# Long convolution with real and imaginary parts on one partition, in 64x32 and 32x64 pieces of the array

## The chip, the cores and the metric

The kernel runs on one core of one Trainium2 chip. The metric is the time of one execution in microseconds (us), the median of several timed runs. A separate execution was taken by the hardware profiler; its trace and its page are what is read here.

## The reference

Two independent heads are computed and put side by side, 1024 columns each, for 2048 time steps.

Head A is a long convolution with gates:

```python
k_shift = sum over t of k_pad[:, t:t+S, :] * shift_k[:, ks-1-t]     # four taps
kv = k_shift * v
y_f = rfft(kv padded to 2S) * rfft(ssm_k padded to 2S)
y = irfft(y_f)[:S] + kv * ssm_D
a = q * y
```

Head B is a linear recurrence with a diagonal complex state:

```python
Bu = einsum("bld,pd->blp", x, B_bar)          # B_bar complex, 1024 x 1024
h  = Lam_bar * h + Bu[:, t, :]                # 2048 steps, one after the other
y  = 2.0 * einsum("blp,dp->bld", hseq, Cmat).real + x * Dskip
```

All inputs and the output are bf16.

## The kernel before, in words

**Order.** The work of both heads is cut into small tasks, and a long string, ORDER, lists every task in an order fixed beforehand: `name.arguments@engine:slots`. The loop at the end of `full_kernel` calls the tasks in that order. Each engine works through its own instructions in this order; there is no other scheduler. `@G` or `@S` sets the queue of a transfer (G for POOL's, S for SP's; `@D` and `@G` choose VectorE or GpSimd for a copy), and `:a3` or `:d0d1` name the buffers that the task takes: rings a and b in SBUF, e for the spectrum products, w for weights, m for products on VectorE; in PSUM p0 and p1 (one bank each) and d0 to d2 (two banks each). A task that takes a buffer waits until the last user of it is done.

**Head B.** B is loaded (`bl`), transposed on TensorE (`bT`, L458) and copied (`bc`); C and x come by transposing transfers (`cx` L480, `x` L483), on SP's queue. For each of 16 blocks of 128 steps: `U` (L492) multiplies x with B, `ue` copies it, `r1` (L506), `r2`, `sc` (the scan, L523), `r3`, `r4` run on VectorE, `y` (L546 and L551) multiplies with C and D, `ye` and `yst` bring it out. `cm` carries the state from block to block.

**Head A.** The convolution of 4096 points is a product of a transform of 128 points and one of 32. Sequence positions are laid out as 128 partitions x 16 rows.
- `kp` and `vp` load k and v; `kvm`, `kva`, `kvb`, `kvc` make kv on VectorE.
- `am` (L610) is kv's first stage: for row r and half u one matmul per half of the columns, with the 128x128 block matrix F1t, half of which is zero (the two interleaved halves of the sequence do not mix). `ae` copies, `ast` writes to the DRAM array Ys_kv.
- `hl`, `hT`, `hc`, `hm` (L643), `he`, `hst` do the same for the filter ssm_k, into Ys_h.
- For each of 16 groups gq: `lh`, `lk` load the groups back in another layout. `sh` and `sk` (`s2`, L676) are the second stage, four pieces of 64 rows x 64 columns each; `she` and `ske` copy to hab and x16. Real and imaginary parts of a frequency lie on different partitions, 32 apart. `sw` exchanges these halves of hab with four transfers from SBUF to SBUF. `pr` (L704) multiplies on VectorE: x16 with hab and with the exchanged hab. `sa` (L717) is the inverse, again in pieces of 64x64, two accumulated for each result; `sae` copies, `vst` writes to the DRAM array Vs.
- `vl` loads rows of Vs, `a3` (L744) is the output stage with Gt (two accumulated matmuls for each half of the columns), `a3e` copies, `qm` multiplies with q (`qp` loads it), `ost` writes out.

Of the kernel before, what the change touches and what calls it, by code (L numbers as in the profile page):

```python
# [16 lines left out]
BF16 = mybir.dt.bfloat16  # L17
# [10 lines left out]
def a_constants():  # L28
# [4 lines left out]
    G1 = np.zeros((2, 2, 32, 2, 64, 2))  # L33
    for h in range(2):
        F1[:, h, :, h] = np.transpose(F, (0, 2, 1, 3))
        G1[h, :, :, :, :, h] = np.transpose(F, (1, 3, 2, 0)) * (2 / NFFT)
# [5 lines left out]
    WF = np.zeros((2, N2, 2, 32, 3, N2))  # L42
# [3 lines left out]
    WF[:, :, :, :, 2, :] = WF[:, :, :, :, 0, :]  # L46
    WI = np.zeros((2, 2, N2, 16, 2, 2, N2, 2))
    for gi in range(2):
        for ui in range(2):
            for gq in range(16):  # L50
                cc = np.transpose(c_[ui, 2 * gq + gi], (1, 0)); ss = np.transpose(s_[ui, 2 * gq + gi], (1, 0))
                o = WI[gi, :, :, gq, ui]
                o[0, :, 0, :, 0] = cc; o[0, :, 0, :, 1] = ss
                o[1, :, 0, :, 0] = -cc; o[1, :, 0, :, 1] = -ss
                for cp in range(2):
                    o[cp, :, 1, :, 0] = -ss; o[cp, :, 1, :, 1] = cc
    W = np.concatenate([WF.reshape(128, NWP, 4 * 96), WI.reshape(128, NWP, 2 * 256)], axis=2)
    f = lambda a: np.ascontiguousarray(a.reshape(128, -1), dtype=np.float32).astype(ml_dtypes.bfloat16)
    return f(F1), f(G1), f(W)
# [3 lines left out]
NA = 11  # L63
# [6 lines left out]
wb.7:p1 bc.5.1 par_rest vp.0@G:a10 ld_G@S sin2 wb.4:p0 cx.5.1 wbe.4 sin1 wb.6:p0 cx.0.0 wbe.6@D eo.0 bl.3.1:b3 wb.1:p0 wbe.7@D bl.1.0:b4 wbe.1@D  # L70
wb.2:p1 cx.0.1 eo.1 stt.0 wb.0:p0 cx.7.0 wbe.2 stt.1 eo.3 wb.5:p1 bl.3.0:b6 x.1:b2 wbe.5@D wbe.0 stt.3 wb.3:p1 wbe.3 bT.6.1:p0 cx.1.0 dd bT.2.0:p1
kvm.0:m0 vp.1:a1 vp.2:a0 cx.6.0 bc.6.1 cx.6.1 bT.0.1:p0 bc.2.0 bc.0.1@D kp.2@G eo.2 bT.2.1:p1 kva.0 hT.0.0:p0 hc.0.0:b8 stt.2 bc.2.1 hT.0.1:p0
bT.7.1:p1 hc.0.1:b13 kvb.0:a7 bc.7.1 hT.0.6:p0 hm.0.0.1:d0 kvc.0 hc.0.6:b10 hT.0.3:p1 hm.0.0.0:d1 kvm.4:m0 he.0.0.1:b5 am.1.1:d2 hc.0.3:b11
hm.0.6.1:d0 hst.0.0.1 hT.0.2:p0 bT.0.0:p1 he.0.6.1:b8 hc.0.2:b0 hst.0.6.1@S cx.1.1 bc.0.0 bT.7.0:p0 bc.7.0@D cx.3.1 z1 U.0.3.0:p1 kva.4 hm.0.6.0:d0
U.0.3.1 cx.3.0 U.0.2.0:p0 kvb.4:a8 U.0.2.1 ue.0.3:a10 he.0.6.0:b7 kvm.2:m0 bT.1.0:p1 bc.1.0 am.0.1:d0 bT.3.0:p1 ue.0.2 bc.3.0 bT.3.1:p0 bc.3.1
U.0.0.0:p1 U.0.0.1 he.0.0.0:b5 kp.4@G kva.2 kp.3@G ae.0.1:b10 hm.0.3.1:d1 U.2.2.0:p0 ue.0.0 ast.0.1@S vp.4:a5 kvc.4 U.0.1.0:p1 ae.1.1:b4 cx.5.0
hm.0.1.0:d0 he.0.3.1:b6 ast.1.1 kvb.2:a6 hm.0.3.0:d2 hst.0.6.0 U.0.1.1 he.0.1.0:b3 hst.0.3.1 kvc.2 U.2.2.1 ue.0.1 hst.0.1.0 he.0.3.0:b11 U.1.2.0:p1
r1.0:m0 ue.2.2:a0 hst.0.3.0@S hm.0.1.1:d1 hst.0.0.0@S am.4.0:d0 he.0.1.1:b8 cx.2.0 U.2.1.0:p0 r2.0:a1 U.1.2.1 U.2.1.1 ue.1.2:a10 kvm.8:m0 U.1.1.0:p1
ue.2.1 ae.4.0:b13 hm.0.2.0:d2 am.4.1:d1 z2 ast.4.0 am.0.0:d0 U.2.3.0:p0 hst.0.1.1 ae.4.1:b4 U.1.1.1 he.0.2.0:b7 ast.4.1@S sc.0 U.2.3.1 ue.1.1
hst.0.2.0@S hm.0.2.1:d1 cx.7.1 ue.2.3 am.5.1:d2 ae.0.0:b6 hT.0.4:p1 cx.2.1 am.2.0:d0 hc.0.4:b10 ast.0.0 U.1.0.0:p0 ae.2.0:b3 hT.0.7:p1 cx.4.0 kva.8  # L80
U.1.0.1 ue.1.0 hT.0.5:p0 hc.0.7:b0 hl.5:a9 kvb.8:a4 hl.4:a2 U.2.0.0:p1 hc.0.5:b13 ast.2.0@S hl.7:a3 r3.0:m0 U.1.3.0:p0 he.0.2.1:b8 am.1.0:d0 hst.0.2.1
hm.0.5.0:d1 U.1.3.1 cm.0:a7 kvc.8 U.2.0.1 ue.1.3 he.0.5.0:b11 r4.0 U.4.0.0:p0 ue.2.0 hm.0.4.0:d1 r1.1:m0 U.4.0.1 he.0.4.0:b5 U.4.2.0:p1 ue.4.0:a5
hst.0.4.0@S ae.5.1:b6 hm.0.7.1:d1 r2.1 U.4.2.1 ae.1.0:b4 ast.5.1 U.4.1.0:p0 hl.6@G:a10 r1.2:m0 he.0.7.1:b7 ast.1.0@S hst.0.5.0 am.8.1:d2 ue.4.2
U.4.1.1 hm.0.5.1:d0 sc.1 am.5.0:d1 he.0.5.1:b8 U.4.3.0:p1 ue.4.1 am.2.1:d0 ae.5.0:b3 y.0.0.0:p0 ae.2.1:b13 hm.0.4.1:d1 hm.0.7.0:d0 ast.2.1@S U.4.3.1
x.3:b6 he.0.7.0:b10 r2.2:a0 am.8.0:d0 ae.8.1:b5 hst.0.7.0 y.0.0.1 r3.1:m0 hst.0.5.1 ue.4.3 ast.8.1@S ast.5.0@S y.0.0.2 ae.8.0:b0 vp.3:a8 y.0.1.0:p1
ast.8.0 cm.1 hst.0.7.1 r4.1 am.3.0:d2 y.0.1.1 ae.3.0:b4 r1.4:m0 y.0.0.3 ast.3.0 ye.0.0:b11 hT.1.4:p0 y.0.1.2 sc.2 hc.1.4:b13 he.0.4.1:b10 hT.1.3:p0
hm.1.4.1:d0 am.9.0:d2 hc.1.3:b9 hst.0.4.1@S ae.9.0:b8 hT.1.5:p0 am.9.1:d1 y.0.1.3 he.1.4.1:b5 r2.4:a5 am.3.1:d2 ye.0.1 hst.1.4.1 hm.1.3.1:d0
y.1.1.0:p1 he.1.3.1:b0 kvm.6:m0 hc.1.5:b3 y.1.1.1 hst.1.3.1@S ae.3.1:b7 hT.1.7:p0 y.1.1.2 ae.9.1:b4 hm.1.4.0:d0 hm.1.5.1:d2 hc.1.7:b10 ast.9.1 y.1.1.3
kp.6 kva.6 hT.1.6:p0 ast.9.0@S ye.1.1:b5 kp.5 hm.1.7.0:d1 hc.1.6:b13 yst.0@S y.1.0.0:p1 ast.3.1@S he.1.5.1:b0 hT.1.1:p0 cm.2:a4 kvb.6:a1 y.1.0.1
hst.1.5.1 hc.1.1:b4 lw.1@G:w0 hm.1.6.0:d2 r3.2:m0 y.1.0.2 he.1.6.0:b2 y.1.0.3 he.1.4.0:b8 hst.1.6.0@S hT.1.0:p0 r4.2 ye.1.0 hst.1.4.0 hm.1.6.1:d2  # L90
hm.1.3.0:d0 he.1.6.1:b13 vp.6@G:a6 U.3.2.0:p1 kvc.6 yst.1 he.1.7.0:b9 hst.1.6.1 hm.1.1.0:d2 kvm.12:m0 U.3.2.1 hc.1.0:b0 hst.1.7.0@S x.7:b11
hm.1.7.1:d1 y.2.0.0:p0 he.1.7.1:b10 x.6:b7 he.1.1.0:b8 y.2.0.1 hm.1.0.0:d1 hst.1.1.0@S hm.1.1.1:d2 he.1.0.0:b2 y.2.0.2 kva.12 ue.3.2:a7 am.6.1:d1
# [54 lines left out]
def full_kernel(ctx, tc, A_q, A_k, A_v, A_shift_k, A_ssm_k, A_ssm_D, B_x, B_Lre, B_Lim, B_Bre, B_Bim,  # L147
# [235 lines left out]
    def kv_space():  # L383
# [45 lines left out]
    def kx(b):  # L429
        nc.sync.dma_start_transpose(st["kT"][:, b, 4:4 + S], k[:, b * P:(b + 1) * P])  # L430
# [393 lines left out]
```

## Time and profile before

| | |
|---|---|
| median of 3 timed runs | 385.99 us (381.66 to 388.22) |
| profiled execution, its own time | 380.41 us |
| its span, first to last instruction | 378.5 us |
| granted TensorE clock | 1.000 |
| busy: TensorE, VectorE, ScalarE, GpSimd | 92%, 86%, 70%, 21% |
| DMA packets, bytes | 67418, 100.06 MB |
| U (L492), y (L546), one-block-of-D (L551) | 127.7, 127.7, 28.0 us busy on TensorE |
| hm (L643), am (L610), a3 (L744) | 20.6, 19.0, 16.1 us |
| second stage (L676), inverse (L717) | 256 matmuls each; 22.1 and 18.2 us |
| transposes of B and of the filter (L458, L630) | 13.9, 12.5 us |

How to read it: PE is TensorE's matmuls, PEld its weight loads, DVE VectorE, ACT ScalarE, POOL GpSimd, SP SyncE, which only issues transfers here. A matmul's busy time contains its way through the pipeline: of matmuls that follow each other, the starts tell the pace, not the durations. Where a row names a releaser ("<-DMA ld"), the engine sat idle until this had come.

### The profile page before, as it was taken

Reading aid. Unit: us, or ns where it says so; the run is one execution under the profiler, and the core shown is the slowest. Engines: PE = TensorE matmul, PEld = TensorE weight load, DVE = VectorE, ACT = ScalarE, POOL = GpSimd, SP = SyncE. Lnnn points to the kernel's source line nnn. Section 1 sums busy time; section 2 is a strip of 40 time slices with the busy share of each in tenths; the row PEclk is TensorE's granted clock in tenths of the full one; section 3 lists DMA queues with packets and bytes.
Section 4 is the critical chain, followed back from the end, with each engine's and each line's share of the span. In section 5 each row is a group of like instructions: output and inputs, shape, how many; then the busy total and the mean of one; then the engine's idle time right before and its main releaser. Section 6 shows DMA issues by size and latency. Waiting matters only on the chain.

```text
span 378.5 us, 8748 instructions
## 1 busy us (share of the span) xinstructions
PE 346.6 (92%) x3661; PEld 225.6 (60%) x3661; DVE 324.6 (86%) x229; ACT 264.2 (70%) x341; POOL 81.3 (21%) x150
## 2 busy tenths in 40 slices
PE   4548889899899999999999999989999999999995
PEld 3226678785455578855444757367867664467442
DVE  6989599999999997999997797576899999993972
ACT  4978798877778886952785879778869771346433
POOL 7300023022112521214200325330210202211021
PEclk9999999999999999999999999999999999999999
DMA  6999999997578999999999897999989539877995
GB/s 231 317 338 216 265 272 286 296 314 235 200 243 270 247 313 287 281 272 268 190 275 312 258 324 234 220 267 221 284 236 312 175 125 325 306 229 255 350 319 206
DMA packets 67418, 100.06 MB, mean 264 GB/s; under 512 B 38435, under 2 KB 42147, under 8 KB 67380
## 3 DMA queue, kind: packets, MB, share of 16 engines
q1 hardware_dynamic: 54660, 56.32, 54.8%
q0 software_dynamic: 12720, 43.19, 36.8%
q8 instruction: 28, 0.46, 0.5%
q14 instruction: 10, 0.08, 0.1%
HBM read 49.16 MB, written 33.55 MB: 219 GB/s over the span
## 4 chain that ended last, share of the span: by engine, by line
PE 56%; DMA 15%; issue 13%; ACT 7%; SPq 4%; POOL 2%; DVE 1%; POOLq 0%; ACTq 0%; DVEq 0%
PE ps_u L492 22%; PE ps_y L546 16%; PE ps_a L744 4%; DMA wts<-a_c_W 4%; SPq L483 4%; DMA Ys_kv<-ysb 3%; PE ps_a L643 3%; DMA l2k<-Ys_kv 3%; DMA ld<-in_B_B_re_dram 3%; PE ps_a L717 3%; PE ps_a L610 3%; DMA hab<-hab 2%; PE ps_a L676 2%; PE ps_t L630 2%; ACT ysb L615 2%
## 5 line engine op out<-in xcount | busy, mean ns | idle before, releaser
L492 PEld LDWEIGHTS <-BT 128*128 128x128 bf16 x2048 | 119.3, 98 | 22.6 <-issue 11.7
L492 PE MATMUL ps_u<-xT,BT 128*128 128x128 bf16 x2048 | 127.7, 219 | 2.4 <-ACT u L497 1.2
L546 PE MATMUL ps_y<-CT,h 128*128 128x512 bf16 x512 | 127.7, 379 | 0.0
L546 PEld LDWEIGHTS <-h 128*128 128x128 bf16 x512 | 44.6, 98 | 48.0 <-issue 6.1
L523 DVE TENSOR_TENSOR_SCAN h<-rtab,h 128x2080 bf16<-128x2080 f32 x16 | 71.8, 4488 | 0.2
L497 ACT CAST u<-ps_u 128x512 bf16<-128x512 f32 x64 | 38.2, 603 | 27.0 <-PE ps_u L492 19.1
L506 DVE TENSOR_TENSOR mt<-u,Z 128x4096 bf16<-128x4096 bf16 x16 | 36.7, 2291 | 15.8 <-ACT u L497 15.4
L704 DVE TENSOR_TENSOR hab<-x,hab 128x4096 bf16<-128x4096 bf16 x16 | 36.5, 2286 | 15.2 <-DMA hab<-hab 10.5
L556 ACT CAST yo<-ps_y 128x512 bf16<-128x512 f32 x32 | 19.1, 596 | 28.0 <-PE ps_y L546 24.4
L650 ACT CAST ysbh<-ps_a 128x1024 bf16<-128x1024 f32 x32 | 32.3, 1033 | 8.8 <-PE ps_a L643 7.5
L691 ACT CAST x<-ps_a 128x1024 bf16<-128x1024 f32 x32 | 31.9, 1026 | 8.8 <-PE ps_a L676 5.9
L506 DVE TENSOR_TENSOR mt<-h,Z 128x4096 bf16<-128x4096 bf16 x16 | 36.7, 2292 | 0.5
L724 ACT CAST vsb<-ps_a 128x1024 bf16<-128x1024 f32 x32 | 31.7, 1027 | 6.5 <-PE ps_a L717 6.0
L583 DVE TENSOR_TENSOR mt<-kring,wbc 128x2048 bf16<-128x2048 bf16 (+3 forms) x14 | 35.8, 2592 | 0.4 <-ACT wbc L473 0.2
L615 ACT CAST ysb<-ps_a 128x1024 bf16<-128x1024 f32 x32 | 32.3, 1043 | 2.7 <-issue 1.6
L685 ACT CAST hab<-ps_a 128x1024 bf16<-128x1024 f32 x32 | 32.2, 1030 | 2.1 <-PE ps_a L676 1.9
L551 PE MATMUL ps_y<-Dd,xT 128*128 128x128 bf16 x128 | 28.0, 219 | 0.0
L749 ACT CAST ot<-ps_a 128x1024 bf16<-128x1024 f32 x16 | 15.7, 1018 | 14.1 <-PE ps_a L744 14.1
L169 POOL DMA_DIRECT2D Ys_h<-ysbh x20 | 14.3, 716 | 43.3 <-ACT ysbh L650 43.3
L168 POOL DMA_DIRECT2D hab<-hab x32 | 15.6, 494 | 32.1 <-ACT hab L685 18.3
L458 PE MATMUL ps_t<-ident,ld 128*128 128x128 bf16 x128 | 13.9, 285 | 9.1 <-DMA ld<-in_B_B_re_dram 4.4
L643 PE MATMUL ps_a<-hT,F1t 128*128 128x512 bf16 x64 | 20.6, 402 | 0.8 <-ACT ysbh L650 0.6
(116 smaller groups left out, 381.8 us busy)
## 6 DMA issues: line engine op xcount, KB each, us to landing
Ys_h<-ysbh POOLq DMA_DIRECT2D x20, 256.0 KB, 5.5
l2h<-Ys_h SPq DMA_DIRECT2D x9, 512.0 KB, 9.7
Vs<-vsb SPq DMA_DIRECT2D x9, 512.0 KB, 4.3
vv<-Vs SPq DMA_DIRECT2D x9, 512.0 KB, 5.2
Ys_kv<-ysb POOLq DMA_DIRECT2D x17, 256.0 KB, 6.2
l2k<-Ys_kv SPq DMA_DIRECT2D x8, 512.0 KB, 3.9
hab<-hab SPq DMA_DIRECT2D x32, 128.0 KB, 5.4
l2k<-Ys_kv POOLq DMA_DIRECT2D x8, 512.0 KB, 7.8
```

Source lines behind the costliest of these rows:

```text
L492: nc.tensor.matmul(pu[:, w, jl, :], BT[:, 2 * jp + jl, w, d, :], xT[:, d, :], start=(d == 0), stop=(d == ND - 1))
L497: nc.scalar.copy(u[:, :, 2 * jp:2 * jp + 2, :], st["pu", i, jp][:])
L506: nc.vector.tensor_mul(m, s_, w_)
L523: nc.vector.tensor_tensor_scan(gf, rtab[:].rearrange("p a j t -> p (a j t)"), gf, 0.0, ALU.mult, ALU.add)
L546: nc.tensor.matmul(py[:], h[:, 1 - w, j, 2:TP], CT[:, j, w, dh * 512:(dh + 1) * 512], start=(j == 0 and w == 0), stop=(j == NJ - 1 and w = ...
L583: nc.vector.tensor_mul(m[:, :, j0:j0 + n, :], a_, wbc[:, j0:j0 + n, :].unsqueeze(1).to_broadcast([P, 2, n, DV]))
L615: nc.scalar.copy(st["ysb", r, u][:], st["pa", r, u][:].rearrange("p e d -> p (e d)"))
L643: nc.tensor.matmul(pd[:, e, :], F1t[:, u, :], st["hT", f, rp][:, e, :], start=True, stop=not sk)
L650: nc.scalar.copy(st["yh", f, rp, u][:], st["pa", f, rp, u][:])
L685: nc.scalar.copy(hab[:, a, :, e * 512:(e + 1) * 512], st["ps", key, gq, e][:])
L691: nc.scalar.copy(x16[:, :, e * 512:(e + 1) * 512], st["ps", "k", gq, e][:])
L704: nc.vector.tensor_mul(hab, x16.unsqueeze(1).to_broadcast([P, 2, 2 * D]), hab)
```

## The change

- **Layout of the sequence.** Position n*32 + h*16 + s lies on partition 64h + n (before: 2n + h), for k, v, q and the output. The transfers of k, v, q take rows of 4 KB as before; the two early tasks `kp.-1` and `kp.-2` are cut at 64 and 63 partitions instead of 112 and 15.
- **kv's first stage.** `am` does both halves u and both halves h of the sequence for half the columns, as four pieces of 64x64 (FK is the new part of F1t, without zeros). `ysb` is one tile for a row r now, with 4 KB a partition, in ring a; `ast` is split by h instead of u.
- **Second stage.** `s2` makes one part (ri: real or imaginary) for all columns, in eight pieces of 64 rows x 32 columns. The real and the imaginary part of a frequency then lie on the same partition. There is no `sw`.
- **Product.** `pr` multiplies the two parts of hab with the two parts of x16, four products of 1024 elements: as many elements as before.
- **Inverse.** `sa` makes both halves of the columns at once, in four steps of eight pieces of 32 rows x 64 columns, and takes two of the buffers d0 to d2. The weights have three blocks instead of two (wts: 1024 columns instead of 896).
- **Output stage.** `a3` has, for each half of the columns, two matmuls of 128 rows x 64 columns side by side instead of two accumulated ones of 128x128. `vl` is split in two transfers.
- **Order.** The whole of ORDER is new, with one more buffer in ring a (NA = 12). Which copies go to VectorE, and which transfers to which queue, changes with it.

```diff
-NA = 11
+NA = 12
...
-ld_par bl.4.0@G:b0 bl.5.0@G:b1 bl.5.1@G:b2 bl.4.1:b3 bl.6.0:b4 bl.2.1@G:b5 ld_sd@S bl.1.1@G:b6 ld_w@S:a0a1 kp.0@G kp.-2 ld_F par_T:p0 hl.2@G:a2
-bl.7.0:b7 bT.4.0:p1 p32 exp1 bl.6.1:b8 hl.3@G:a3 bc.4.0 dve2 x.0:b9 kp.-1@G bT.5.0:p0 dve3 sm_pre bT.4.1:p1 bc.5.0 hl.1@G:a4 bl.0.1:b10 bc.4.1
-bl.7.1@G:b11 x.4:b12 bT.6.0:p0 tabA1:a5a6a7a8 bc.6.0 bl.2.0:b13 hl.0:a9 exp2 bl.0.0:b0 sin0 rt@G kp.1 bT.1.1:p1 x.2:b1 bT.5.1:p0 tabA2 bc.1.1 cx.4.1
+ld_par bl.2.0@G:b0 bl.4.1@G:b1 ld_F bl.0.1:b2 ld_sd@S:b3 bl.2.1@G:b4 hl.3:a0 bl.5.1@G:b5 ld_w@S:a1a2 bl.7.0@G:b6 kp.-1 hl.1@G:a3 par_T:p0 bl.6.0@G:b7
+bl.7.1:b8 bT.2.0:p1 p32 bl.5.0:b9 bl.4.0@G:b10 exp1 cx.4.1 dd dve2 kp.-2@G dve3 bc.2.0@D kp.0@G bl.1.1:b11 sm_pre hl.0@G:a4 bT.2.1:p0 hl.2@G:a5
...
-    kr = k.rearrange("(n s) d -> n s d", s=NR)
+    kr = k.rearrange("(n h s) d -> h n s d", h=2, s=NR)
...
-    def am(r, u):
+    def am(r, e):
         pd = dtile("ps_a")
-        st["pa", r, u] = pd
-        for e in range(2):
-            nc.tensor.matmul(pd[:, e, :], F1t[:, u, :], kvt(r)[:, r % 2, e * 512:(e + 1) * 512], start=True, stop=True)
+        st["pa", r, e] = pd
+        for h in range(2):
+            hp = slice(64 * h, 64 * h + 64)
+            for u in range(2):
+                nc.tensor.matmul(pd[64 * u:64 * u + 64, h, :], F1t[hp, 256 + 64 * u:320 + 64 * u],
+                                 kvt(r)[hp, r % 2, e * 512:(e + 1) * 512], start=True, stop=True, tile_position=(64 * h, 64 * u))
...
-    def s2(key, nm, gq, e, o):
+    def s2(key, nm, gq, ri):
...
         for gi in range(2):
-            for u in range(2):
-                up = slice(64 * u, 64 * u + 64)
-                b0 = ((2 * gq + gi) % 4) * 96 + 32 * o
-                nc.tensor.matmul(pd[64 * gi:64 * gi + 64, u, :], wt[up, b0:b0 + 64],
-                                 st[nm, gq][up, gi, e * 512:(e + 1) * 512], start=True, stop=True,
-                                 tile_position=(64 * u, 64 * gi))
+            b0 = ((2 * gq + gi) % 4) * 64 + 32 * ri
+            for e in range(2):
+                c_ = 32 * (2 * gi + e)
+                for u in range(2):
+                    up = slice(64 * u, 64 * u + 64)
+                    nc.tensor.matmul(pd[c_:c_ + 32, u, :], wt[up, b0:b0 + 32], st[nm, gq][up, gi, e * 512:(e + 1) * 512],
+                                     start=True, stop=True, tile_position=(64 * u, c_))
...
-    def sw(gq):
-        hab = st["hab", gq]
-        for b in range(4):
-            o = b ^ 1
-            spd(hab[32 * b:32 * b + 32, 1, :, :], hab[32 * o:32 * o + 32, 0, :, :])
-    E["sw"] = sw
...
     def pr(gq):
-        hab = st["hab", gq][:].rearrange("p a u d -> p a (u d)")
-        x16 = st["x16", gq][:].rearrange("p u d -> p (u d)")
-        nc.vector.tensor_mul(hab, x16.unsqueeze(1).to_broadcast([P, 2, 2 * D]), hab)
+        hab = st["hab", gq][:].rearrange("p a b u d -> p a b (u d)")
+        x16 = st["x16", gq][:].rearrange("p b u d -> p b (u d)")
+        nc.vector.tensor_mul(hab, hab[:, :, 1:2, :].to_broadcast([P, 2, 2, D]), x16.unsqueeze(1).to_broadcast([P, 2, 2, D]))
...
-    def sa(gq, e):
+    def sa(gq):
         wt = st["w", gq // 2]
         hab = st["hab", gq]
-        pd = dtile("ps_a")
-        st["ps", "v", gq, e] = pd
-        for a in range(2):
-            for u in range(2):
-                for gi in range(2):
-                    gp = slice(64 * gi, 64 * gi + 64)
-                    b0 = 4 * 96 + (gq % 2) * 256 + u * 128 + a * 64
-                    nc.tensor.matmul(pd[64 * u:64 * u + 64, gi, :], wt[gp, b0:b0 + 64],
-                                     hab[gp, a, u, e * 512:(e + 1) * 512], start=(a == 0), stop=(a == 1),
-                                     tile_position=(64 * gi, 64 * u))
+        pds = [dtile("ps_a") for _ in range(2)]
+        for a, b, n in ((0, 0, 0), (0, 1, 2), (1, 0, 2), (1, 1, 1)):
+            for gi in range(2):
+                for e in range(2):
+                    st["ps", "v", gq, e] = pds[e]
+                    cp = slice(32 * (2 * gi + e), 32 * (2 * gi + e) + 32)
+                    for u in range(2):
+                        b0 = 4 * 64 + (gq % 2) * 384 + u * 192 + n * 64
+                        nc.tensor.matmul(pds[e][64 * u:64 * u + 64, gi, :], wt[cp, b0:b0 + 64], hab[cp, a, b, u, :],
+                                         start=(a + b == 0), stop=(a + b == 2), tile_position=(32 * (2 * gi + e), 64 * u))
...
-    def vl(r):
-        st["vv", r] = k4("vv", [P, 2, D])
-        spd(st["vv", r][:], Vs[:, r, :, :].rearrange("u k d -> k u d"))
+    def vl(r, h):
+        vv = once(("vv", r), lambda: k4("vv", [P, 2, D]))
+        spd(vv[:, h, :], Vs[:, r, 64 * h:64 * h + 64, :])
...
         for e in range(2):
-            for u in range(2):
-                nc.tensor.matmul(pd[:, e, :], Gt[:, u, :], st["vv", r][:, u, e * 512:(e + 1) * 512], start=(u == 0), stop=(u == 1))
+            for h in range(2):
+                nc.tensor.matmul(pd[64 * h:64 * h + 64, e, :], Gt[:, h, :], st["vv", r][:, h, e * 512:(e + 1) * 512],
+                                 start=True, stop=True, tile_position=(0, 64 * h))
```

More of the change, by code (lines that the diff above doesn't have):

```diff
@@ L52, in a_constants @@
                 o = WI[gi, :, :, gq, ui]
[L53 to L57, printed above, removed]
+                o[:, :, 0, :, 0] = cc; o[:, :, 0, :, 1] = ss
+                o[:, :, 1, :, 0] = -cc; o[:, :, 1, :, 1] = -ss
+                o[:, :, 2, :, 0] = -ss; o[:, :, 2, :, 1] = cc
@@ L73 @@
[L73 to L80, printed above, removed]
@@ L657, in lw @@
     def lw(w):
-        st["w", w] = rtile(ring, "w", "wts", [P, 4 * 96 + 2 * 256])
+        st["w", w] = rtile(ring, "w", "wts", [P, 4 * 64 + 2 * 384])
         spd(st["w", w][:], Wv[:, w, :])
@@ L686, in full_kernel, with she, ske @@
+    E["sh"] = lambda gq, ri: s2("h", "l2h", gq, ri)
+    E["sk"] = lambda gq, ri: s2("k", "l2k", gq, ri)
+    def she(gq, ri):
+        hab = once(("hab", gq), lambda: k8("hab", [P, 2, 2, 2, 512]))
+        nc.scalar.copy(hab[:, ri, 1, :, :], st["ps", "h", gq, ri][:])
     E["she"] = she
-    E["sxe"] = lambda gq, e: she(gq, e, "x", 1)
-    def ske(gq, e):
-        x16 = once(("x16", gq), lambda: k4("x16", [P, 2, D]))
-        nc.scalar.copy(x16[:, :, e * 512:(e + 1) * 512], st["ps", "k", gq, e][:])
+    def ske(gq, ri):
+        x16 = once(("x16", gq), lambda: k4("x16", [P, 2, 2, 512]))
+        nc.scalar.copy(x16[:, ri, :, :], st["ps", "k", gq, ri][:])
```

215 lines of the change are left out of this document (110 added, 105 removed).

## The prediction

> **What bounds the kernel now.** I read the page first (busy time by engine, chain of waits), then the windows, then the timeline of TensorE where it changes between whole-array and piece work, then the timeline at the start.
>
> ```profile
> PE 346.6 (92%) x3661; PEld 225.6 (60%) x3661; DVE 324.6 (86%) x229; ACT 264.2 (70%) x341; POOL 81.3 (21%) x150
> ```
> TensorE is busy for 92% of the span. The windows (length, then busy time and instructions of PE, PEld, DVE, ACT and POOL, the granted clock, the DMA share and GB/s) tell where the other 8% lie:
>
> ```profile
> 0.00:10.00 10.00, 4.11 (x33) 3.34 (x33) 6.97 (x22) 5.17 (x6) 7.11 (x19) 1.00 0.69 237
> 10.00:20.00 10.00, 5.36 (x22) 2.32 (x23) 9.43 (x29) 9.09 (x18) 3.45 (x7) 1.00 1.05 310
> 20.00:30.00 10.00, 5.05 (x37) 3.63 (x37) 8.26 (x12) 7.69 (x21) 0.53 (x1) 1.00 1.15 339
> 30.00:40.00 10.00, 8.72 (x50) 5.10 (x49) 9.53 (x10) 6.88 (x8) 0.74 (x1) 1.00 1.08 219
> 40.00:50.00 10.00, 7.92 (x106) 6.79 (x105) 6.09 (x4) 8.41 (x10) 0.00 (x0) 1.00 1.14 276
> ...
> 250.00:300.00 50.00, 47.55 (x709) 35.56 (x707) 42.51 (x21) 40.71 (x51) 6.75 (x13) 1.00 0.93 255
> 300.00:350.00 50.00, 49.86 (x459) 29.91 (x456) 41.43 (x25) 24.83 (x33) 7.83 (x12) 1.00 0.69 233
> ```
> In the first 50 us TensorE works 31.2 us (the sum of the five rows) and idles 18.8. From 50 to 350 us it idles 9.3 us in all (the six windows of 50 us). So what counts is how much TensorE work there is, how early it can start, and a few waits in between. A group of the page that the change touches (busy time, mean ns, idle time before it and what ended it):
>
> ```profile
> L704 DVE TENSOR_TENSOR hab<-x,hab 128x4096 bf16<-128x4096 bf16 x16 | 36.5, 2286 | 15.2 <-DMA hab<-hab 10.5
> ```
> And four pieces of the chain of waits (start, duration, what):
>
> ```profile
> 205.42 0.56 PE ps_a L676 x8
> ...
> 207.84 0.99 PE ps_a L717 x16
> ...
> 213.62 0.77 PE ps_a L676 x12
> ...
> 323.38 0.86 PE ps_a L744 x4
> ```
> A full-array matmul of 512 columns takes a place of 0.216 us (four in 0.86). Pieces of 64x64 take the same place four at a time: 8, 12 and 16 of them last 0.56, 0.77 and 0.99 us, that is 0.216 us for each round of four and 0.126 us over. Ahead of a stretch of pieces the trace has another gap: the last U matmul starts at 205.202, its successor would start 0.056 later, the first piece starts at 205.351, which is 0.093 us more; nearly all 34 visits show this 0.093. So a visit to piece work costs 0.219 us, plus 0.216 us a round.
>
> **The change, part by part.** The sum is made against the profiled execution: 380.41 us, of which the span is 378.5; it lies 1.4% under the median of the timed runs, 385.99, so that a result of the sum is multiplied by 1.0147 at the end.
>
> (1) First stage of kv (am, L610). Before: 64 matmuls in place of 0.216 = 13.8 us. After: 128 pieces of 64x64 = 32 rounds = 6.9 us. The built order of the changed kernel puts them in 28 visits (24 of one round, 4 of two): 28 x 0.219 = 6.1 us. Sum -0.8 us: alone in its visit, one am costs 0.435 us against 0.432. Nearly nothing is won.
>
> (2) Output stage (a3, L744). Before 64 x 0.216 = 13.8 us. After, 64 matmuls of 128 rows by 64 columns, two column halves at a time if they run as the 64x64 pieces with the same rows do (these start 2 to 4 ns apart): 32 places = 6.9 us, and 16 visits = 3.5 us. Sum -3.4 us. If they don't run together: +3.5 us. I take -3.4, since two column halves side by side are what the pieces of L676 are already.
>
> (3) Second stages (L676) and inverse (L717). Before: 512 pieces in fours = 128 rounds = 27.6 us, and 39 visits in the built order = 8.5 us. After: 1024 pieces (64x32 and 32x64), by eights again 128 rounds, and 42 visits (26 and 16) = 9.2 us. Sum +0.7 us if eight run at once, as four do; +27.6 more if only four do (13.8 for each of the two kinds). No row shows more than four at once. The nearest is the round itself: starts 1.6 to 3.5 ns apart, and the next round 0.216 later, so issue leaves room for eight (8 x 3.5 = 28 ns). What is not seen is four streams into the same rows, and four accumulators written at the same time. I take eight at once.
>
> The Trainium skill (TensorE: Matmul & The Clock Gate, Part 3: Packing small matmuls) says that small tiles run concurrently, about 4 ns a tile, up to sixteen. By that page the term is +0.7, by the row's cautious reading +28.3; no run here shows eight yet.
>
> (4) The exchange goes. 64 transfers of 128 KB (8.4 MB of the page's 100 MB) leave the queues: 32 from SP, 32 from POOL (15.6 us of issue there). VectorE waited 10.5 us for them in four products, but it is not the bound: TensorE lost 0.7 us to the product behind it, 2.3 to weights (wts) and 0.7 to l2h loads that shared the DMA. The product keeps its size and its 2.29 us (both operands are repeated, as in the r1 products of L506, 2.29 us too). ScalarE's copies keep count and size; only three copies of BT (0.69 us each) go to VectorE and two of wbc to ScalarE. Of those 3.7 us I take 2 as won: -2 us; the ends are -9 (all idle time of 50 to 350) and +16.5, from the next point.
>
> (5) The inverse now holds two of the three big accumulators at once (before one), and each is freed by a ScalarE copy of 1.03 us. Behind it in TensorE's order stand mostly U and y matmuls, which use the small accumulators, so I take 0. If each of the 16 waited for one copy: 16 x 1.03 = +16.5 us; for both, +33. Queued behind such a wait is everything on TensorE.
>
> (6) The new order at the start, where the trace shows this (SP's queue and TensorE's waits):
>
> ```profile
> 6.99 4.90 SPq L483 DMA_TRANSPOSE xT<-in_B_x_dram  x1
> ...
> 12.71 8.41 SPq L483 DMA_TRANSPOSE xT<-in_B_x_dram  x1
> 21.17 0.58 SPq L168 DMA_DIRECT2D ld<-in_B_B_re_dram  x1
> ```
> ```profile
> 11.70 1.89 PE L458 MATMUL ps_t<-ident,ld 128*128 128x128 bf16 x16 [2.48 <-DMA ld<-in_B_B_im_dram]
> ...
> 26.83 1.89 PE L458 MATMUL ps_t<-ident,ld 128*128 128x128 bf16 x16 [3.68 <-DMA ld<-in_B_B_re_dram]
> ```
> Two x transposes keep SP's queue for 13.3 us, B loads stand behind them, and TensorE waits 2.5 and 3.7 us for B. The changed order has 7 transposes ahead of the first U matmul (before 14: 4 of x, 10 of C), and 12.3 MB of transfers instead of 14.5. At the mean 286 GB/s of 10 to 50 us, 2.1 MB are 7.4 us; the two waits are 6.2 us. But POOL's queue now has 17 transfers ahead of the first product of kv instead of 12 (0.53 us each, +2.7), and the last three B loads stand behind the table copies (2.0 us) and four other loads, so U of step 0 may wait for them. I take -5 us; the ends are -12 and +3.
>
> Other parts: k, v, q and output rows are still pieces of 4 KB or 2 KB, and vv loads are split in two (16 issues of about 0.5 us more, in the last third, where the DMA share is 0.69): 0. The weights grow from 224 to 256 KB a load: 0.25 MB in all: 0.
>
> **Sum**: -0.8 - 3.4 + 0.7 - 2 - 5 = -10.5 us: 369.9 us in a profiled execution, 375 us as a median, 2.8% under before.
>
> **Rivals.** (B) The start and the transfers give more: -3.5 - 10 - 6 = -19.5, 366 us. For it: DMA share over 1.0 from 10 to 50 us. Against: after 50 us little idle time is left to win. (C) Start and transfers give nothing, as the products of kv on VectorE (9.43 and 9.53 us busy in two of the first windows) hold it back: -3.5, 382 us. (D) The other side: eight pieces do not run at once. It decides from 82 ns more a round on (10.5 us / 128 rounds); at four at a time for both kinds it is -10.5 + 27.6 = +17.1: 403 us, for one kind 389. Against it: issue leaves room; for it: nothing in the trace shows four streams a row. (E) The pair of accumulators: +16.5 to +33 as in (5), net +6 to +22, middle 400 us. For it: in 250 to 300 us TensorE already idles 2.45 us and ScalarE is busy 81%; against: the order has other work between. That the change does not do what it says gets no chance: the built program has no exchange, and the counts are those above.
>
> **How the numbers follow.** The measurement of this kernel tells about 2% from no change (its three runs differ by 1.7%). The forecast has 0.46, with its own range 366 to 384 (0.39 faster, 0.07 within 2%); B 0.12 (faster); C 0.12 (0.08 within 2%, 0.04 slower with a late B load on top); D 0.15 (0.12 slower, 0.03 within, one kind only); E 0.15 (0.12 slower, 0.03 within). That is 0.51, 0.21, 0.28. The range 362 to 396 holds the forecast, C, most of B and the lower ends of D and E.
>
> **What would show it.** Right: rounds of eight 0.216 us apart in L681 and L713; a3 0.65 us in a visit; first U before 40 us (44.1 before); PE busy about the same while the span is shorter. Wrong: a distance of 0.3 us or more between rounds (D); TensorE waiting for copies of vsb ahead of L713 (E); first U at 44 us or later (C).

## Result and profile after

The changed kernel takes 676.72 us (median of 4 runs, 665.95 to 684.48); the kernel before, beside it on the same chip, takes 383.83 us (378.63 to 388.22). The ratio is 1.761, 95% interval 1.711 to 1.812. Executions of one kernel fall into a fast and a slower group a few per cent apart, and every ratio with an interval compares the fast ones alone, so it can differ a little from the ratio of two medians. The forecast was 375 us, 2.8% faster: 302 us short. The profiled execution took 684.48 us where the sum for it said 369.9. Its first U matmul starts at 85.0 us (44.1 before).

The page of the changed kernel, busy time and the DMA's packets, queues and chain:

```profile
PE 392.7 (58%) x4237; PEld 239.6 (35%) x4237; DVE 325.8 (48%) x230; ACT 264.1 (39%) x340; POOL 97.4 (14%) x146
...
DMA packets 99729, 92.22 MB, mean 135 GB/s; under 512 B 72885, under 2 KB 76997, under 8 KB 99686
...
q1 hardware_dynamic: 50134, 44.06, 46.6%
q0 software_dynamic: 49552, 47.54, 33.6%
...
DMA 56%; PE 18%; SPq 9%; issue 6%; ACT 4%; POOL 2%; DVE 1%; POOLq 0%; ACTq 0%; DVEq 0%
```

The same two rows of the kernel before:

```profile
DMA packets 67418, 100.06 MB, mean 264 GB/s; under 512 B 38435, under 2 KB 42147, under 8 KB 67380
...
PE 56%; DMA 15%; issue 13%; ACT 7%; SPq 4%; POOL 2%; DVE 1%; POOLq 0%; ACTq 0%; DVEq 0%
```

VectorE and ScalarE are as busy as before (324.6 and 264.2 us), but their shares of the span have nearly halved: they have no more work, they wait. The chain of waits is 56% DMA where it was 15%. The kernel moves 8 MB less than before (92.22 MB against 100.06), at half the rate (135 GB/s against 264).

Is TensorE's 46 us more of busy time (392.7 against 346.6) more work? Not most of it: U keeps its 2048 matmuls and goes from 127.7 to 139.5 us, y its 512 and from 127.7 to 152.9, and the granted clock is 0.828 where it was 1.000. In the runs below the clock comes back as TensorE is fed again (0.72 in `e7_all_on_sp` at 893 us, 0.840 in `e3_loads_only` at 596, 0.906 in `e4_stores_only` at 511, 0.974 in `e1_one_level` at 415), so I read the lower clock as following the waits; no run sets the clock by itself.

The windows of the changed kernel (length, then busy time and instructions of PE, PEld, DVE, ACT, POOL, the granted clock, the DMA share, GB/s) show where it starts:

```profile
10.00:20.00 10.00, 6.55 (x43) 4.17 (x43) 6.29 (x23) 7.89 (x11) 3.75 (x5) 1.00 1.07 259
20.00:30.00 10.00, 5.56 (x29) 2.88 (x29) 6.77 (x20) 7.43 (x21) 1.37 (x2) 1.00 1.44 108
30.00:40.00 10.00, 2.05 (x16) 1.77 (x17) 5.85 (x2) 0.71 (x1) 1.16 (x4) 1.00 1.53 149
```

From 20 us on the DMA counts as busier than before (1.44 and 1.53, against 1.15 and 1.08 in the prediction's windows) and moves 108 and 149 GB/s instead of 339 and 219. A high share with a low rate says that the engines hold packets without moving many: from 20 to 30 us a 4 KB packet of POOL's queue is held for 389 ns on the mean, 161 before. Which transfers? The trace's list of DMA issues (KB each, median us from issue to landing; rows without a median have no landing the profile could pair), first the changed kernel, then the kernel before:

```profile
vv<-Vs POOLq DMA_DIRECT2D x19, 256.0 KB, 23.9
...
kring<-in_A_k_dram POOLq DMA_DIRECT2D x7, 512.0 KB, 27.1
...
qt<-in_A_q_dram POOLq DMA_DIRECT2D x7, 512.0 KB, 20.6
...
v<-in_A_v_dram POOLq DMA_DIRECT2D x6, 512.0 KB, 31.0
l2k<-Ys_kv POOLq DMA_DIRECT2D x6, 512.0 KB, 4.8
```
```profile
vv<-Vs POOLq DMA_DIRECT2D x7, 512.0 KB, 5.2
...
kring<-in_A_k_dram POOLq DMA_DIRECT2D x5, 512.0 KB, 6.6
...
v<-in_A_v_dram POOLq DMA_DIRECT2D x4, 512.0 KB, 5.4
...
qt<-in_A_q_dram POOLq DMA_DIRECT2D x2, 512.0 KB, 4.5
```

The l2k load, whose form the change does not touch, lands in 4.8 us (7.8 before on this queue). The loads of k, v, q and Vs rows, which it does touch, take 4 to 6 times as long as before for the same bytes (Vs rows 4.6 times as long for half of them). Some untouched transfers that share the queue with them are late too: the filter's loads (hk) land in 23.6 us instead of 11.4, its stores to Ys_h in 15.5 instead of 5.5. In `e7_all_on_sp` below, where POOL's queue no longer has these loads and stores, the two land in 10.7 and 6.2 us again. What the loads that the change does touch have in common is written in the diff: their 128 rows in DRAM are now named by two strides, an outer dimension of 2 and an inner one of 64 (`"h n s d"`, `Ys_kv[:, r, 64 * h:64 * h + 64, :]`), where they had one stride over 128.

The packets of the trace show what this does. The output store that POOL issues at 647.01 us has 64 packets of 4 KB (two strides); they start between 648.58 and 655.26, a median of 91 ns apart, and on the mean 1.94 of them are under way at once. In the kernel before, 128 such packets, of two stores with one stride issued 0.6 us apart, start between 372.41 and 374.15, 8 ns apart, and 11.7 are under way at once. SP's queue shows it with single transfers: in the changed kernel the 2 KB packets of its output stores between 655 and 667 us start 43 ns apart, 2.08 at once; in the kernel before, the last store on this queue, with the DMA to itself (128 packets of 2 KB, 376.13 to 376.87 us), has them 5 ns apart and 13.3 at once. So these stores of two strides are served two packets at a time, whether the packets have 4 KB or 2.

The Trainium skill has this as a rule (DMA: Bandwidth & Descriptors, section Why a DMA increments its semaphore by 16 and not by 1): a transfer runs on the largest number of engines, up to 16, that divides the outermost dimension of both sides. An outermost 2 gives two engines. The 1.94 and 2.08 packets at once agree.

### The profile page after: what moved, and what is told of

Read it like the earlier page. It is cut to its first block, busy times and chain, and to the rows that moved or that the text cites. A ratio compares the mean times of both kernels' runs of the same rounds, so it can differ in the third digit from the quotient of the medians.

```text
span 682.6 us, 9797 instructions
## 1 busy us (share of the span) xinstructions
PE 392.7 (58%) x4237; PEld 239.6 (35%) x4237; DVE 325.8 (48%) x230; ACT 264.1 (39%) x340; POOL 97.4 (14%) x146
## 2 busy tenths in 40 slices
DMA packets 99729, 92.22 MB, mean 135 GB/s; under 512 B 72885, under 2 KB 76997, under 8 KB 99686
## 4 chain that ended last, share of the span: by engine, by line
DMA 56%; PE 18%; SPq 9%; issue 6%; ACT 4%; POOL 2%; DVE 1%; POOLq 0%; ACTq 0%; DVEq 0%
DMA xT<-in_B_x_dram 11%; DMA vv<-Vs 9%; DMA Ys_h<-ysbh 7%; PE ps_u L491 7%; DMA out_dram<-ot 6%; DMA Ys_kv<-ysb 6%; SPq L479 6%; DMA ld<-in_B_B_re_dram 6%; PE ps_y L545 5%; DMA l2h<-Ys_h 5%; DMA Vs<-vsb 3%; SPq L168 2%; DMA out_dram<-yo 2%; PE ps_a L681 2%; PE ps_a L713 2%
## 5 line engine op out<-in xcount | busy, mean ns | idle before, releaser
L491 PE MATMUL ps_u<-xT,BT 128*128 128x128 bf16 x2048 | 139.5, 229 | 56.8 <-DMA xT<-in_B_x_dram 41.3
L545 PE MATMUL ps_y<-CT,h 128*128 128x512 bf16 x512 | 152.9, 431 | 15.6 <-ACT hT L638 11.4
L491 PEld LDWEIGHTS <-BT 128*128 128x128 bf16 x2048 | 128.4, 103 | 79.9 <-DMA xT<-in_B_x_dram 42.3
L545 PEld LDWEIGHTS <-h 128*128 128x128 bf16 x512 | 49.3, 109 | 81.2 <-issue 46.9
L699 DVE TENSOR_TENSOR hab<-hab,x 128x4096 bf16<-128x4096 bf16 x16 | 36.6, 2287 | 30.8 <-ACT x L693 27.6
L749 DVE TENSOR_TENSOR ot<-ot,qt 128x1024 bf16<-128x1024 bf16 x16 | 10.3, 686 | 83.1 <-DMA qt<-in_A_q_dram 58.8
L739 PE MATMUL ps_a<-vv,Gt 128*64 128x512 bf16 x64 | 14.6, 510 | 54.0 <-DMA vv<-Vs 49.5
L618 ACT CAST ysb<-ps_a 128x1024 bf16<-128x1024 f32 x32 | 31.9, 1024 | 16.7 <-PE ps_a L612 11.2
L550 PE MATMUL ps_y<-Dd,xT 128*128 128x128 bf16 x128 | 32.3, 252 | 0.0
L612 PE MATMUL ps_a<-acc,F1t 64*64 64x512 bf16 x128 | 14.1, 439 | 31.5 <-ACT ysbh L653 31.4
L638 ACT COPY hT<-ps_t 128x1024 bf16<-128x1024 bf16 x16 | 16.1, 1015 | 39.8 <-PE ps_t L633 19.5
## 6 DMA issues: line engine op xcount, KB each, us to landing
Ys_h<-ysbh POOLq DMA_DIRECT2D x16, 256.0 KB, 15.5
```

What stands on the lines that cost most here:

```text
L491: nc.tensor.matmul(pu[:, w, jl, :], BT[:, 2 * jp + jl, w, d, :], xT[:, d, :], start=(d == 0), stop=(d == ND - 1))
L545: nc.tensor.matmul(py[:], h[:, 1 - w, j, 2:TP], CT[:, j, w, dh * 512:(dh + 1) * 512], start=(j == 0 and w == 0), stop=(j == NJ - 1 and w = ...
L550: nc.tensor.matmul(py[:, dl * P:(dl + 1) * P], st["xT", i][:, d, :], Dd[:, d, :], start=False, stop=False)
L618: nc.scalar.copy(ysb[:, :, e * 512:(e + 1) * 512], st["pa", r, e][:])
L699: nc.vector.tensor_mul(hab, hab[:, :, 1:2, :].to_broadcast([P, 2, 2, D]), x16.unsqueeze(1).to_broadcast([P, 2, 2, D]))
```

## Experiments

Sixteen kernels. "Before" is always the kernel before, run beside them on the same chip: 379 us in the first two groups, 381, 379 and 378 us later.

### 1. Is it the two strides, and which transfers?

`e1_one_level`: the changed kernel; every load of k, v, q and every output store becomes two transfers of 64 partitions with one stride, and the Ys_kv stores and Vs loads are cut by u instead of h, which has one stride.

```diff
-            spd(t_, kr[:, :, 2 * r:2 * r + 2, :].rearrange("h n s d -> h n (s d)"))
+            for h in range(2):
+                spd(t_[64 * h:64 * h + 64, :, :], kr[h, :, 2 * r:2 * r + 2, :])
...
-        spd(vv[:, h, :], Vs[:, r, 64 * h:64 * h + 64, :])
+        spd(vv[64 * u:64 * u + 64, :, :], Vs[u, r, :, :].rearrange("(h k) d -> k h d", h=2))
```

> The changed kernel, its order, layout and computation kept; only the transfers whose 128 partitions are addressed by two strides (h and n, or u and k) are cut into pieces with one stride: loads of k, v, q and the store of the output in two transfers of 64 partitions each, the stores to Ys_kv and the loads of Vs regrouped by u instead of h (as many as before). Theory 1, the two-stride transfers on POOL's queue are slow in themselves: the 17920 packets of 8 bytes and some 17900 of 4 bytes go, k loads land in about 7 us instead of 27, and the time falls from 677 to 365 to 400 us. Theory 2, the new order (which queue carries what, and when) starves the engines: still over 600 us. Theory 3, the layout with h ahead of n is slow for the memory, however it is addressed: still over 600 us.

Measured 417.11 us (413.4 to 423.43) against 379.04: of the 298 us between 379.04 and the changed kernel's 676.72, 260 are gone. Theories 2 and 3 fall; theory 1 has the cause, but the time lies above its 365 to 400 us (group 3 asks why).

`e2_layout_alone`: the kernel before with only the four access patterns of k, v, q and the output changed to the two-stride form.

> The kernel before with its own order, pieces and exchange; only k, v, q and the output of head A are addressed with h ahead of n as in the changed kernel, in two-stride transfers (11 loads of 512 KB and 7 stores of 256 KB of them on POOL's queue). The tables are left as they were, so the rows of kv meet coefficients of other rows: the work is the same, the values are not. Theory 1: 11 x 896 packets of 4 bytes and 7 x 448 of 8 bytes appear and the time rises by 100 us or more, to 480 to 600 us. Theory 2 (the new order): no change, 375 to 390 us. Theory 3 (the layout): rises like theory 1.

559.72 us (554.99 to 564.44) against 379.04. So 181 us come with the layout's transfers alone, in the order and with the arithmetic of before.

`e3_loads_only` and `e4_stores_only`: the changed kernel with only the loads of k, v, q, or only the Ys_kv stores, Vs loads and output stores, in one-stride form.

> The changed kernel with only the loads of k, v and q cut into two transfers with one stride; Ys_kv, Vs and the output stay two-stride. Theory 1: the packets of 4 bytes fall by 17920, those of 8 bytes stay; the first 100 us run at the pace of before (first U matmul near 40 us), the stretches with Ys_kv stores and Vs loads stay slow: 480 to 580 us. Theories 2 and 3: over 600 us.

> The changed kernel with only the stores to Ys_kv and the output and the loads of Vs in one-stride form; the loads of k, v and q stay two-stride. Theory 1: the packets of 8 bytes go, those of 4 bytes stay; the last third runs at the pace of before, the first U matmul stays late (about 70 us or later): 480 to 580 us. Theories 2 and 3: over 600 us.

595.75 us (ratio 1.575, 1.555 to 1.596) and 509.58 us (1.348, 1.329 to 1.367). Against 676.72 that is 81 and 167 us; together 248 of the 260. Both groups cost by themselves; they hardly hide each other. (e3 lies above the 480 to 580 us expected of it: its group is the smaller one.)

`e7_all_on_sp`: the changed kernel, two strides kept, but all these transfers on SP's queue. On POOL's queue each two-stride 512 KB load comes with 896 packets of 4 bytes, each 256 KB store with 448 of 8 bytes; on SP's there are none.

> The changed kernel with all two-stride transfers on SP's queue, still two-stride: the loads of k (from block 0), v, q and Vs, the stores to Ys_kv and the output. Theory 1a, the small packets of 4 and 8 bytes that POOL's queue makes of them are the cost: they are gone, and the time falls to 400 to 450 us (SP's queue is longer). Theory 1b, a two-stride transfer goes through one of the sixteen engines in place of all, on either queue, and the small packets only go with it: no small packets, and still over 600 us.

892.85 us (one run). The page, packets and queues of this run:

```profile
DMA packets 65609, 92.00 MB, mean 103 GB/s; under 512 B 36205, under 2 KB 40317, under 8 KB 65566
...
q1 hardware_dynamic: 57934, 65.03, 41.0%
q0 software_dynamic: 7632, 26.35, 9.5%
```

The packets under 512 B have fallen from 72885 to 36205, fewer than before the change, and it is still slower: the little packets are not needed for the loss. (What they add on POOL's queue, no run shows.) The form itself is the cost, on either queue. That one queue with two packets at a time is worse than two such queues is how I read the 893 us against 677. My expectation spoke of one engine; the packet times above say two.

### 2. Were the steps on TensorE right?

They can be read in `e1_one_level`, where TensorE is fed. Its timeline:

```profile
265.66 1.29 PE L715 MATMUL ps_a<-hab,wts 32*64 32x512 bf16 x32
...
269.83 0.41 PE L683 MATMUL ps_a<-l2k,wts 64*32 64x512 bf16 x8
```
```profile
378.33 0.62 PE L742 MATMUL ps_a<-vv,Gt 128*64 128x512 bf16 x4
...
381.22 0.62 PE L742 MATMUL ps_a<-vv,Gt 128*64 128x512 bf16 x4 [1.26 <-ACT ot L748]
```

L683 is the second stage, L715 the inverse, L742 the output stage. The starts of the eight pieces of a round lie about 3 ns apart; the rounds of the inverse start at 0, 240, 456 and 672 ns, 216 apart but for the first. From first piece to the next full-array matmul an output stage takes 0.555 us, with the 0.093 ahead of it 0.648; kv's first stage takes 0.343 + 0.093 = 0.436.

### 3. Where are the other 38 us?

First the layout: `e8_layout_in_halves` is the kernel before with the changed layout, and with every such transfer as two halves of 64 partitions.

```diff
-        spd(st["v", r][:], vr[:, 2 * r:2 * r + 2, :])
+        for h in range(2):
+            spd(st["v", r][64 * h:64 * h + 64, :, :], vr[h, :, 2 * r:2 * r + 2, :])
```

> The kernel before, with its order and its arithmetic untouched, and the changed layout alone, as in e2_layout_alone, but with every load of k, v and q and every store of the output cut into two transfers of 64 partitions with one stride each. Its tables were left as they were, so the order of the sequence in its result is another; the amount of work is the same. Open after e1_one_level: its 417 us are 38 us over the kernel before, and its first U starts 23 us later. Theory X: the rest is the new order alone, the layout costs next to nothing once the form with two strides is gone: some 40 issues more of 0.5 us, spread over two queues that wait for nothing: 379 to 385 us, first U at 43 to 47 us. Theory Y: transfers over 64 partitions only, or twice as many of them, are themselves slower and hold up the start: 395 us or more, first U later than 50 us.

395.91 us against 381.38, ratio 1.057 (1.040 to 1.074). Theory X falls: by the interval the halves cost 15 to 28 us by themselves. Theory Y has the time; the first U, which it put later than 50 us, came at 49.4. Its timeline of TensorE at the start has the wait that the prediction showed with 3.68 us at 26.83:

```profile
32.90 1.89 PE L458 MATMUL ps_t<-ident,ld 128*128 128x128 bf16 x16 [9.46 <-DMA ld<-in_B_B_re_dram]
```

TensorE waits 5.8 us longer for this load of B, with the same order; U matmul 512 of 2048 (counted from 0) then starts at 127.0 instead of 116.7 us.

Then the order: `e12_new_order_old_layout` is the changed kernel with the layout of before (whole-array kv first stage and output stage, one stride over 128 partitions); left are the exchange's removal, the Vs loads in two transfers (each over 128 partitions) and the new order.

> The changed kernel with the layout of before: k, v, q and the output with one stride over 128 partitions, kv's first stage and the output stage as whole matmuls as before (ysb still one tile for a row, cut by half u, and vv loaded by half u in two transfers). What is left of the change: second stage, product and inverse without an exchange, and the whole new order. Theory P: the new order is itself slow at the start (in e1_one_level the first U came at 67 us instead of 44), and the halves of the layout cost the rest (16 to 22 us as in e8_layout_in_halves): 417 - 16 to 22, plus 4 for the whole matmuls = 399 to 405 us. Theory Q: the prediction's steps 3, 4 and 6 are right where the transfers land as in the kernel before: +0.7 - 2 - 5 = 373 us, first U before 40 us; the whole loss of e1_one_level then comes from the halves.

400.49 us against 378.94, but the four runs are 386.05, 400.39, 400.59 and 404.89: all above every run of the kernel before (375.22 to 380.69), by anything from 7 to 26 us. Theory Q's 373 us falls; whether the loss has the size that theory P says, this kernel's runs alone leave open. The trace is of the 400.39 us. In it the first U comes at 43.0 us (44.1 before; theory Q asked for earlier than 40), so it is not the first U that is late. The loss lies behind it: U matmul 512 starts at 129.4 us instead of 116.7, and up to there TensorE is as busy as before (93.9 us against 93.7) and idles 35.5 us instead of 23.1. The halves (15 to 28 us) and the order (7 to 26 here, 15 in the steadier e12d below) are together of the size of the 38 us; the two were not run against each other more closely than that.

Can the start be mended? Three runs moved transfers in `e1_one_level`, whose first U is at 67.2 us because it waits 14.9 us for x.

- `e6_x0_early`: x.0 right behind the first transposes of B.
- `e6b_c_late`: besides, eight of the cx behind the first U.
- `e6c_pool_relieved`: besides, six loads on SP's queue instead of POOL's.

> e1_one_level with a single task moved: the transposing load of the first x block stands right behind the fourth transpose of B in the order, ahead of three transposing loads of C on SP's queue instead of behind them. Theory A, the new order's start is late because x stands behind C on SP's queue: TensorE's wait of 14.9 us for xT goes, the first U matmul comes at about 52 us instead of 67, the time falls from 417 to 400 to 405 us. Theory B, the start is bound by the transfers in all, whichever comes first: the wait for xT is taken over by waits for B and the filter, the first U stays at 60 us or later, 410 to 420 us.

> e6_x0_early, and besides eight of the sixteen transposing loads of C (all that stood ahead of U of block 0) moved behind the first U matmuls, spread up to the first y. Theory A: these transposes (9 to 15 us of SP's queue each in e1_one_level) are what slows the start: first U at about 45 us, 385 to 398 us. Theory B: under 5 us from e6_x0_early. If y of block 0 then waits for C, the move gives part of it back.

> e6b_c_late, and besides six early loads (two of the filter, one of v, one of k, two of B) on SP's queue instead of POOL's. Theory C, POOL's queue takes no more than about ten transfers at a time, so that loads far down its list start late (it waited 0.5 to 2.3 us ahead of each from the tenth on in e1_one_level): TensorE's wait of 8 us for the filter goes, first U at 38 to 42 us, 375 to 390 us. Against it: no change from e6b_c_late.

425.68 us (ratio 1.125, 1.116 to 1.133), 403.24 (1.053, 1.045 to 1.061) and 408.99 us. The first U moves to 47.8, 47.5 and 42.3, yet x.0 early alone wins nothing: the 256th U comes at 104.1 us instead of 97.0. The wait was taken over by others: TensorE now waits 16.5 us for later blocks of x, and 15.4 for B instead of 8.0. With C deferred as well it is 14 us under `e1_one_level` by the medians, and TensorE waits 9.8 us for copies of ysbh (L655 there). Loads off POOL gain nothing more. All three times lie above what theories A and C asked for.

`e12b_start_mended` has the two moves of e6b without the halves.

> e12_new_order_old_layout with the two moves of e6b_c_late: x.0 right behind the first transposes of B, eight transposes of C behind the first U. Theory P: these gave 14 us in e1_one_level with the slower loads, and give as much here: 385 to 391 us. Theory Q: its start is already free, they give nothing: 371 to 376 us. If it comes out below 373 it would beat the kernel before.

398.74 us, ratio 1.053 (1.045 to 1.062): no gain, neither theory's time. What it waits for now is plain in its timelines, SP's queue first, then TensorE:

```profile
63.68 0.67 SPq L166 DMA_DIRECT2D Ys_h<-ysbh  x1
64.40 11.67 SPq L477 DMA_TRANSPOSE CT<-in_B_C_re_dram  x2
76.11 4.28 SPq L477 DMA_TRANSPOSE CT<-in_B_C_im_dram  x1
80.48 0.53 SPq L166 DMA_DIRECT2D Ys_kv<-ysb  x1
```
```profile
83.47 1.01 PE L640 MATMUL ps_a<-hT,F1t 128*128 128x512 bf16 x2 [3.06 <-ACT ysbh L647]
...
92.86 1.01 PE L607 MATMUL ps_a<-acc,F1t 128*128 128x512 bf16 x2 [8.38 <-ACT ysbh L647]
```

Transposes of C hold SP's queue for 16 us between two stores of the first stages; the buffers of the copies stay taken, the copies wait, and TensorE waits 11.4 us for the copies. In the kernel before the last of the 16 transposes of C is issued at 73.5 us; in e12 at 106.4, in e12b at 107.9. They now stand in the stretch where these stores run.

`e12c_stores_on_pool` and `e12d_stores_on_pool` move nine of these stores to POOL's queue, in e12b and in e12.

> e12b_start_mended with the nine stores of the first stages (kv and filter) that stand among the transposes of C on SP's queue moved to POOL's queue, which has room there. Theory P2: the new order defers transposes of C from before the first U to 45 to 105 us, where these stores stand behind them on SP (a store issued at 63.7, the next at 80.5, with 16 us of transposes between), the copies' buffers stay taken, and TensorE waits 12 us in 80 to 93 us for ysbh copies; with the stores on the other queue these waits go: 386 to 390 us. Theory R: the stores are late because the DMA itself is full (share 1.15 to 1.23 in 60 to 90 us), whatever the queue: 396 to 401 us.

> e12_new_order_old_layout with the same nine stores moved to POOL's queue. There TensorE waited 7.9 us in 68 to 76 us for an x transpose that stood on SP behind a transpose of C (10.4 us), a store and another transpose of C (10.5 us), and little for copies. Theory P2: a transpose holds SP's queue for some 10 us when it follows a store on it; without the stores between them that wait shrinks: 390 to 395 us. Theory R: the transposes are slow because the DMA is full: 398 to 402 us.

396.77 us (392.49 to 404.77; ratio 1.043, 1.034 to 1.052) and 392.84 us (390.44 to 395.02; ratio 1.040, 1.033 to 1.048). e12d has the time that P2 gave it. TensorE's longest wait of e12 is gone and another has grown, as rows of the two lists of waits show (us in total, times, longest), first e12, then e12d:

```profile
PE ps_u L489 <- DMA xT<-in_B_x_dram: 7.7, 1, 7.7
...
PE ps_a L640 <- ACT ysbh L647: 1.6, 3, 1.2
```
```profile
PE ps_a L639 <- ACT ysbh L646: 5.2, 4, 3.5
```

The last transpose of C is issued at 84.6 us instead of 106.4, and U matmul 512 starts at 121.9 us instead of 129.4. e12c misses P2's 386 to 390, and its median lies in theory R's 396 to 401: its waits for copies of ysbh shrink from 14.0 us to 3.9 (L606 and L639 there), but 4.7 us of waiting for x and 5.0 us before the second stage take their place. The ranges of e12 and e12d overlap, and so do those of e12b and e12c, so the timed runs don't settle whether the queue matters; the traces show waits that went with it and others that came, and I take it as part of the loss, not all. Of the 15 us that e12d keeps over the kernel before, 5 are there by U matmul 512. Behind it TensorE idles 2 us more, and the U and y matmuls, as many as before, are busy for 261.0 us instead of 255.4 over the whole run, at a granted clock of 0.975 instead of 1.000. Why the clock is lower there stays open.

### 4. Is any part worth keeping?

`e9_output_stage_alone`, `e10_no_exchange_alone` and `e11_both` take the change's arithmetic into the order of before: the output stage in pieces (q, output and Vs rows in halves), the second stage and inverse in eights without `sw` (the buffers d0 to d2 dealt anew in turn), and both.

```diff
 e10, ORDER
-... sw.1 ... sa.1.0:d0 sa.1.1:d2 ...
+... sa.1:d0d2 ...
```

> The kernel before, and of the change only the output stage: a3 as two pieces of 128 rows by 64 columns side by side, the loads of Vs rows cut by u into two transfers of 64 partitions (32 instead of 16), q and the output in the changed layout in halves of 64 partitions (16 instead of 8, 32 instead of 16 transfers). Step 2 of the prediction is right: 16 x (0.86 - 0.65) = 3.4 us less on TensorE, whose span in the last 50 us is full: 375 to 377 us where the kernel before has 379. Rival: the last part of the span doesn't shrink, since 40 more issues or the DMA's landing times hold the output rows up, or since ScalarE's copies set the pace: 378 to 384 us.

> The kernel before with its own order and layout, and of the change only the second stage in pieces of 64x32, the product without an exchange (64 transfers of 128 KB less) and the inverse in pieces of 32x64 that holds two of the three big accumulators; the two former tokens of the inverse become one at the place of the second, and the numbers of the big accumulators are dealt anew in turn; two small early tables lie in other memory to make room for the wider weights. Steps 3 and 4 of the prediction: +0.7 - 2 = 1.3 us less, 377 to 379 us where the kernel before has 379, with no wait of TensorE for copies of vsb. Rival E: with two of three accumulators held the second stage of the next group waits for copies of 1.03 us: 6 us or more above the kernel before, with such waits in the trace. Rival F: the exchange costs more than 2 us where it stands: 374 us or less.

> e9_output_stage_alone and e10_no_exchange_alone together: the change's arithmetic of three stages in the order of the kernel before, with the filter's and kv's first stage, k and v as before. If the two gains add: 379 - 3.4 - 1.3 = 374 us, below the kernel before by 1.2%. If the loss of one eats the other's gain: 379 us or more.

Against 381.38: 388.17 us (ratio 1.016, 0.9997 to 1.032), 386.93 (1.025, 1.012 to 1.038), 390.77 (1.036, 1.026 to 1.047). None gains: they lie above the 375 to 377, 377 to 379 and 374 us that a gain would have given. In e9 the timeline of TensorE shows the output stage waiting for rows of Vs, and the list of DMA issues has their landing times:

```profile
365.09 1.05 PE L746 MATMUL ps_a<-vv,Gt 128*64 128x512 bf16 x8 [2.13 <-DMA vv<-Vs]
```
```profile
vv<-Vs SPq DMA_DIRECT2D x18, 256.0 KB, 9.3
```

From the last U matmul to TensorE's end it takes 26.4 us, 25.5 before. TensorE's work there did shrink, from 25.5 us to 24.0 (7 of the 16 visits stand in this stretch), but 2.4 us of idling came, 2.1 of it for transfers that carry half as much and land in 9.3 us (7.0 on POOL's queue) instead of 5.2. More is lost at the two ends: the last U starts 2.4 us later (351.6 against 349.1), and behind TensorE's end the run goes on for 8.8 us instead of 3.9 (8.9 in e11), with output stores, now in halves, issued on SP's queue up to 383.0 us. The Trainium skill advises against such pairs (DMA: Bandwidth & Descriptors, section Rules for kernel authors): two transfers to the two halves of the partitions serialize, one over all 128 is to be used. e8 and e9 agree that such pairs are slower; that the two halves serialize is not read from a trace here.

In e10 TensorE's waits are 1.6 us for copies of vsb (two of 0.8), 2.3 for weights (as before), and 4.0 for copies of ysb and ysbh at the first stages, where dealing the accumulators anew changed who waits for whom (1.3 before). So rival E exists, at a tenth of its price, and the exchange's removal has no gain here to set against it.

## Why the prediction was wrong

The step that failed is the one that had the least argument: **"Other parts: k, v, q and output rows are still pieces of 4 KB or 2 KB ...: 0"**. The row size was right and beside the point. What mattered is how many packets of a transfer are under way at once, 1.9 to 2.1 where a store with one stride had 13.3, and the access patterns in the diff say it: an outermost dimension of 2. Term: 0 predicted, 260 us measured (81 for the loads of k, v and q, 167 for the Ys_kv stores, Vs loads and output together). The Ys_kv stores, cut by h, stood in no term at all, and of the Vs loads only the issues were counted. No rival named it, so the range of 362 to 396 us could not hold it.

The others, by their numbers (the 34 visits that the prediction counts in the trace of before are 39, of which 38 show the 0.093 us; the cost of a visit stays as it was):

- **(1) kv's first stage, -0.8 us:** 0.435 us a visit predicted, 0.436 measured. Right.
- **(2) Output stage, -3.4 us:** 0.65 us predicted, 0.648 measured. Right on TensorE, but not worth it in time: e9 gives no gain, as the layout that it needs makes loads late (2.1 us of waiting for Vs) and the output stores end later (8.8 us behind TensorE instead of 3.9). The step priced the engine and not the transfers that the pieces ask for.
- **(3) Eight pieces at once, +0.7 us:** rounds 216 ns apart. Right; rival D, eight not at once, is excluded.
- **(4) No exchange, -2 us:** not seen (e10 is 1.2 to 3.8% slower, part of it from the accumulators dealt anew). That VectorE's 10.5 us of waiting was not the bound, as the step said, agrees with this: it is gone, and nothing is gained.
- **(5) Two accumulators held, 0:** 1.6 us of waiting in e10, none seen in `e1_one_level`. Rival E at 16.5 us or more is excluded.
- **(6) New order, -5 us:** the second step that failed. In the changed kernel the first U came at 85.0 us. Without the two strides and the halves it comes at 43.0 us, not before 40, and U matmul 512 is 12.7 us late in e12's trace, 5.2 in e12d's. I counted the transposes that leave the queue ahead of the first U as a gain, and not where they go: behind it, on the queue of the stores that free the first stages' buffers. This is part of the loss; the rest stays open. Rival C (the start gives nothing) was the right kind and too small.

## What to carry to other kernels

When a layout changes, read the outermost dimension of every transfer that follows it before any arithmetic: 128 rows split as 2 x 64 on one side of the transfers cost 260 us here, although the bytes and the rows stayed the same; the trace shows it as a high DMA share at a low rate and as packets starting tens of ns apart. Cutting such a transfer in two halves of the partitions mended most of it, not all (15 to 28 us were left in e8). And a transfer that is deferred has to be priced in the queue and the stretch to which it goes.

## What the runs showed of the hardware

- An output store with an outermost dimension of 2 had two packets under way (1.94 on POOL's queue, 2.08 on SP's), one with 128 rows on one stride 13.3 (SP's queue); a 512 KB load of k landed in 27.1 us instead of 6.6.
- On POOL's queue the two-stride form brings 896 packets of 4 bytes for each 512 KB load; POOL's issue of one takes 0.82 us, of a load with one stride 0.55.
- Pieces of 64x32 and of 32x64 run eight at once, at 216 ns a round.
- A transpose of x or C held SP's queue for 1.2 to 8.4 us in the kernel before, for 1.2 to 21.5 in the changed kernel, where its 256-byte packets took 104 ns on the mean (30 before).
